# Retention and gated FFN on one core: attention steps joined to five groups in the 256-token blocks, weight sums moved to the first steps, the v casts of steps 3 to 8 from GpSimd to ScalarE

## The chip, the core and the metric

The kernel runs on one core of one Trainium2 chip. The core has TensorE (PE in the profile; PEld is its loading of weights), VectorE (DVE), ScalarE (ACT), GpSimd (POOL) and SyncE (SP), which only issues transfers. Each engine works through its own instructions in the order in which the program put them and waits at semaphores for the others. The metric is the time of one execution on the device in microseconds (us).

## The reference

```python
def _attn_ref(q, k, v):                      # q, k, v: 8 batches, 8 heads, 576 positions, 64
    scores = scale * np.matmul(q, k.transpose(0, 1, 3, 2))
    gamma = 1.0 - 2.0 ** (-5.0 - np.arange(H))
    Dmat = np.where(rel >= 0, gamma[:, None, None] ** rel[None, :, :], 0.0)
    return np.matmul(scores * Dmat[None, :, :, :], v)

def _moe_ref(x, w_gate, w_val, w_out):       # x: 4608 tokens x 512; d_ff 1536
    gate = 1.0 / (1.0 + np.exp(-(x @ w_gate)))
    return gate * (x @ w_val) @ w_out
```

Attention without softmax, with a decay that only depends on the distance, gives x; x goes through a gated feed-forward layer.

## The kernel before, in words

**Attention in steps.** The decay is put into tables that multiply q and k, so that within 128 positions the scores need only a triangular mask, and what lies further back is carried in a state. The first 768 token columns are made in pairs. The others are made in 30 *steps* `s` (`STEPS`), 128 columns each: step `s` makes columns 768+128s and on. For each step the loads of k, q and v go out on SP (`load_part`, L170, L173), k and q are multiplied with their tables (`cast_qk`, L425, POOL), v is cast to bf16 (`cast_v`, L430), and q and k together are transposed by a transfer (`cross`, L434, tile `T`; SP) or, for the steps in `TURNED` (0, 1, 7), by TensorE (`turn_step`, L616). On TensorE, `scores` (L654) and `products` (L662) of a step fill the tiles `row`; the DVE masks them (`mask`, L669, tile `pt`) and adds up the state (L784 to L790), which ACT casts (`sb`, L631). Later `intra` (L680) and `inter` (L695) of the same step fill the tiles `val`, and ACT copies these into `xT` (L756, L776). All of these are matmuls of 64x64. A `mark` (L703) is two tiny matmuls between those of one kind and the next.

**The feed-forward layer in blocks.** `BLOCKS` are two blocks of 256 token columns (from 512 and from 768), then blocks of 512. A 256 block has 18 units `i`: 12 of `h_units` (L896; `h_g_0`, `h_v_0`, `h_g_2` up to `h_v_10`), 8 matmuls of 128x256 each, then 6 of `op_units` (L1236; tiles `op_0` and `op_1`), 4 matmuls of 128x512 each. ACT takes the sigmoid of each `h_g` (L899), the DVE multiplies the `h_v` into it (L901), ACT copies each `op` out (L928). The `h` tiles go round three PSUM banks, so an `h` unit waits until ACT or the DVE has read the tile three before it. The block from 768 reads the x of steps 0 and 1; the first 512 block reads that of steps 2 to 5, and its sums (`x_sums`, L978) too.

**The order.** It is written out by hand. After each unit of a block the main loop puts down one thing: a piece of what is pending of an attention group, or the next group. Before, `next_slot(s)` put down single groups in the 256 blocks, with the values of step s-1 and the scores of step s (`slot`): steps 0 to 3 in the block from 512, 4 and 5 in that from 768, and then one joined group `slot_of_two` with the values of step 5 and the scores of steps 6 and 7. Each group was followed by its copies and state sums (`after`) as pending pieces and by the casts of a later step (`casts_to`), which also issue loads. `SUMS_AT` says after which units the DVE makes one of the sums of weights that the 512 blocks need.

Of the kernel before, what the change touches and what calls it, by code (L numbers as in the profile page):

```python
# [16 lines left out]
def kernel(  # L17
# [629 lines left out]
    def scores(s, banks=None):  # L647
        t = turned[s]
        row_ps[s] = [pool.tile([P, 2, M, 64], FP32, tag=tag, name=f"row_{s}_{i}")
                     for i, (pool, tag) in enumerate(banks or ROWS)]  # L650
        for m in range(M):
            for y in range(2):
                for j in range(NJ):
                    nc.tensor.matmul(row_ps[s][y][half(j), 0, m, :], lhsT=t[half(y), 1, m, half(j)],  # L654
                                     rhs=t[half(y), 0, m, half(j)], start=True, stop=True, skip_group_check=True)
# [16 lines left out]
    def values(n, name):  # L672
        return [pool.tile([P, n, 64], FP32, tag=tag, name=f"val_{name}_{i}") for i, (pool, tag) in enumerate(VALS)]

    def intra(s, begins=True):
        for kc in range(M):
            for j in range(NJ):
                for x in range(2):
                    h = 2 * kc + x
                    nc.tensor.matmul(val_ps[s][j][half(x), kc, :], lhsT=natural["v", s][half(j), h, :],  # L680
                                     rhs=probs[s][half(j), h // M, h % M, :], start=(begins and kc == 0),
                                     stop=(kc == M - 1),
                                     skip_group_check=True)

    def inter(s, js):


        for u in range(2):
            for y in range(2):
                for j in js[y]:  # L690
                    if before(s, j) is None:
                        continue
                    for x in range(2):
                        m = 2 * u + x
                        nc.tensor.matmul(val_ps[s][j][half(x), 2 * y + u, :], lhsT=before(s, j)[half(y), m, :],  # L695
                                         rhs=turned[s][half(y), 0, m, half(j)], start=False, stop=(u == 1),
                                         skip_group_check=True)

    def mark(pool, tag, **more):

        t = pool.tile([P, 64], FP32, tag=tag, name="mark", **more)
        for y in range(2):
            nc.tensor.matmul(t[half(y)], lhsT=blank[half(y), half(y)], rhs=blank[half(y), half(y)], start=True, stop=True)  # L703

    def slot(s):

        if s > 0:
            val_ps[s - 1] = values(M, s - 1)
            intra(s - 1)
            inter(s - 1, [(0,), (1,)])  # L710
            mark(st_psum, "st")
        scores(s)
        if STEPS[s][1] < LAST:
            products(s)
        if s > 0:
            mark(st_psum, "st")
            inter(s - 1, [(1,), (0,)])
        mask(s)

    ROWS_2 = [(st_psum, "st"), (ffn_psum, "ffn")]  # L720
    glance = consts.tile([P, NJ], FP32)

    def slot_of_two(vals, news):


        if vals:
            both = values(len(vals) * M, vals[0])
            for i, s in enumerate(vals):
                val_ps[s] = [t[:, i * M:(i + 1) * M] for t in both]
                intra(s, i == 0)  # L730
                inter(s, [(0,), (1,)])
            if len(news) == 2:
                mark(*ROWS_2[0])
            else:
                for j in range(NJ):
                    nc.scalar.copy(out=glance[:, j:j + 1], in_=both[j][:, 0, 0:1])
        for s, banks in zip(news, (ROWS, ROWS_2)):
            scores(s, banks)
            if STEPS[s][1] < LAST:
                products(s)  # L740

        def rest():
            for s in vals:
                inter(s, [(1,), (0,)])

        if not news:
            return rest
        rest()
        for s in news:
            mask(s)  # L750
# [19 lines left out]
                    if (s, j) in totals:  # L770
                        keep_state((b, c, j), totals.pop((s, j)), on_act)

    def leave_x(s, j):

        cols = cols_of(s, j)
        nc.scalar.copy(out=x_out(ALL, cols), in_=x_in(val_ps[s][j], cols))  # L776

    def add_state(s, j):

        b, c = STEPS[s]  # L780
# [8 lines left out]
        else:  # L789
            nc.vector.tensor_copy(out=new, in_=p)  # L790
        running[b] = totals[s, j] = new

    def after(s, i):

        makes = STEPS[s][1] < LAST
        to_bf16 = on_act if s < 6 else on_pool
        if i == 0:
            if makes:
                add_state(s, 0)
        else:  # L800
            if s > 0:
                leave_x(s - 1, i - 1)
                if i == 2 and dealt(cols_of(s - 1, 0)):
                    x_sums(at_col[s - 1], False)
            if i == 1 and makes:
                add_state(s, 1)
            if makes and (s, i - 1) in totals:
                b, c = STEPS[s]
                keep_state((b, c, i - 1), totals.pop((s, i - 1)), to_bf16)


    def first_batch_state():

# [17 lines left out]
    def casts_to(s):  # L831
        while done["cast"] <= min(NS - 1, s):
            x = done["cast"]
            loads_to(3 * (x + 1 + (AHEAD[x] if x < len(AHEAD) else 2)))
            cast_qk(x, 1, nc.gpsimd)
            cast_qk(x, 0, nc.vector if x < 2 else nc.gpsimd)
            if x not in TURNED:
                cross(x)
            cast_v(x, on_dve if x == 0 else on_pool)
            done["cast"] += 1  # L840

    cast_part = [0]
# [2 lines left out]
    def next_cast():  # L845
# [15 lines left out]
        n = 3 * x + i - LOADS["begin"] + 1  # L861
        loads_to(min(LOADS["begin"] + n + 12, LOADS["loaded"] + n + n // 3))
        cast_part[0] = (i + 1) % 3

    def next_slot(s):
        slot(s)
        casts_to(s + LEAD_CAST)
        for i in range(3):
            pending.append(lambda i=i: after(s, i))
        if s + 1 == 1:  # L870
            pending.insert(2, lambda: turn_step(s + 1))

    def next_two(vals, news, late):
        rest = slot_of_two(vals, news)
# [206 lines left out]
        return quarter  # L1081

    PLACES = (((1, 1), "g", 0), ((1, 2), "w", 0), ((2, 1), "w", 1), ((2, 2), "g", 1))
    TURN_AT = -1
    JOINED = "g0 w0 g1 w2".split()
    BY_DVE = "w01 w00".split()
    BY_DVE_LAST = "w00".split()
# [437 lines left out]
    weight_sums = [lambda kind=kind, u=u, i=i: w_sums(kind, i, u, nc.vector) for kind, u in (("g", 2), ("w", 2)) for i in (0, 1, 2, 3)]  # L1525
    weight_sums += [lambda u=u, i=i: wo_sums(i, u, 3) for u in range(3) for i in (0, 1, 2, 3)]

    SUMS_AT = {0: (1,3,5,7,8,9,11,12,13,14,15,16,17), 1: (1,3,4,5,7,9,11)}
    SPARE = {}
    for at, kind, u in PLACES:  # L1530
        SPARE.setdefault(at, []).append(lambda kind=kind, u=u: w_sums(kind, 2, u, nc.vector))
    SINGLE = [4, 2]
    pieces = 0
    slots = 0
    valued = -1
    for w, (t0, n) in enumerate(BLOCKS):
        nxt = BLOCKS[w + 1] if w + 1 < len(BLOCKS) else None
        last = last_step(nxt[0] + nxt[1]) if nxt else NS - 1
        end = slots + (SINGLE[w] if w < len(SINGLE) else 0)
        begin = slots  # L1540
        total = 2 * NFC * 4 * n + 12 * 512 * (n // P)
        n_h = NFC if n <= 256 else 2 * NFC
        if n == 512:
            n_h = 0
        gone = 0
        twos = []
        at = end
        while not twos and valued + (end - begin) < last or twos and twos[-1][0][-1] < last:
            vals = list(range((twos[-1][0][-1] if twos else valued + end - begin) + 1, at))
            twos.append((vals, list(range(at, min(at + 2, NS)))))  # L1550
            at = min(at + 2, NS)
        if w < 1:
            twos = []

        for i, cols in enumerate(ffn_units(t0, n, nxt)):
            if i in SUMS_AT.get(w, ()) and weight_sums:
                weight_sums.pop(0)()
            if w == 1 and i == n_h + TURN_AT:
                turn_step(7)
            for x in SPARE.get((w, i - n_h if w == 1 else i), ()):  # L1560
                x()
            gone += cols
            pieces += 1
            if w == 2 and i in (24, 32):
                keeps[0] -= 1
                leave()
            if stores and (nxt is None or w + 2 == len(BLOCKS) and pieces % 4 == 0):
                leave()
            if n > 256 and i % 2 and i < n_h:
                continue  # L1570
            if pending:
                pending.pop(0)()
            elif slots < end and gone * (end - begin) >= (slots - begin) * (total - 5 * 2048):
                next_slot(slots)
                valued = slots - 1
                slots += 1
            elif twos and (cue if n == 512 else i - n_h >= 1):
                cue.clear()
                next_two(*twos[0], n == 512)
                valued = twos[0][0][-1]  # L1580
                slots = max([slots] + [s + 1 for s in twos.pop(0)[1]])
        assert not twos and slots >= end
        while pending:
            pending.pop(0)()
    while stores:
# [30 lines left out]
```

## Time and profile before

| | us |
|---|---|
| runs | 305.58 median of 3 (304.92, 305.58, 307.17) |
| the profiled execution | 305.17 |
| its span, from the first to the last instruction of the program | 303.5 |
| start of the block from 512 in the chain of waits | 52.43 |
| start of the block from 768 | 71.54 |
| start of the first 512 block | 90.33 |

The span's clock starts with the first instruction; 1.67 us of the profiled execution lie around it. A row of the chain of waits counts a run of matmuls from the end of the one before it where they follow each other without a break, so that successive rows add up; a row of the timeline begins where the first of the matmuls began, up to 0.2 us earlier, since they overlap.

### The profile page before, as it was taken

How to read it: one execution, taken by the hardware profiler on the slowest of the kernel's cores; microseconds unless marked ns; L12 is line 12 of the kernel's file. 1: busy time of each engine (PE TensorE's matmuls, PEld its weight loads, DVE VectorE, ACT ScalarE, POOL GpSimd, SP SyncE). 2: the span in 40 equal slices, each digit the busy share in tenths (PEclk: the TensorE clock that was granted, in tenths of full speed). 3: DMA queues.
4: the chain of work that ended last, by engine and by line, in shares of the span. 5: the costliest groups of instructions: out<-in, count | busy, mean ns of one | idle time of the engine just before them, and what ended most of it. 6: DMA issues, size and time to landing. Idle time of an engine off the chain costs nothing.

```text
span 303.5 us, 10861 instructions
## 1 busy us (share of the span) xinstructions
PE 295.1 (97%) x4433; PEld 243.6 (80%) x4442; DVE 243.8 (80%) x476; ACT 197.1 (65%) x422; POOL 209.5 (69%) x255
## 2 busy tenths in 40 slices
PE   7899999999999999999999999999999999999994
PEld 6764455876858888888888888888888888888883
DVE  5956996787887899689978997898789968946793
ACT  6755463545548656965796579657965886648640
POOL 4776563655367899769976997699769916741670
PEclk9999999999999999999999999999999999999999
DMA  7999999999999995999589929994970390012004
GB/s 214 291 361 402 364 301 215 192 221 177 143 245 211 234 254 133 245 233 248 120 209 244 193 58 196 224 221 65 223 171 2 106 246 3 2 60 84 1 2 138
DMA packets 144994, 55.01 MB, mean 181 GB/s; under 512 B 124336, under 2 KB 136880, under 8 KB 144944
## 3 DMA queue, kind: packets, MB, share of 16 engines
q1 hardware_dynamic: 144144, 53.66, 74.3%
q8 instruction: 35, 0.57, 0.8%
q10 hardware_dynamic: 800, 0.66, 0.7%
q14 instruction: 15, 0.12, 0.1%
HBM read 37.75 MB, written 9.44 MB: 155 GB/s over the span
## 4 chain that ended last, share of the span: by engine, by line
PE 90%; SPq 4%; DMA 2%; DVE 1%; issue 1%; POOL 0%
PE gatea L1020 12%; PE wa L1020 12%; PE qa L1134 11%; PE qe L1134 9%; PE gatee L1020 6%; PE we L1020 6%; PE h_v L896 4%; PE h_g L896 4%; PE op L1476 3%; PE op L1236 3%; PE gateg L1020 3%; SPq L184 3%; PE wg L1020 3%; PE hv L1326 3%; PE hg L1326 3%; PE val L680 2%
## 5 line engine op out<-in xcount | busy, mean ns | idle before, releaser
L425 POOL TENSOR_TENSOR qk<-k,ktab 128x512 bf16<-128x512 f32 x30 | 32.2, 1072 | 17.0 <-DMA k<-in_k_dram 13.7
L1134 PEld LDWEIGHTS <-gsum 128*128 128x128 bf16 x336 | 31.9, 98 | 5.0 <-DVE gsum L957 0.8
L957 POOL TENSOR_TENSOR gsum<-gv 128x256 bf16<-128x256 bf16 (+1 forms) x35 | 26.5, 765 | 12.3 <-DVE gv L1045 11.1
L1020 PEld LDWEIGHTS <-wg_sb 128*128 128x128 bf16 x308 | 30.1, 98 | 3.7
L1020 PEld LDWEIGHTS <-wv_sb 128*128 128x128 bf16 x308 | 30.1, 98 | 3.5
L425 POOL TENSOR_TENSOR qk<-q,qtab 128x512 bf16<-128x512 f32 x28 | 30.7, 1095 | 2.2 <-DMA q<-in_q_dram 2.1
L1020 PEld LDWEIGHTS <-wvt 128*128 128x128 bf16 x280 | 27.4, 98 | 3.2
L1020 PEld LDWEIGHTS <-wgt_sb 128*128 128x128 bf16 x252 | 24.7, 98 | 2.9
L669 DVE TENSOR_TENSOR pt<-row,tri 128x256 bf16<-128x256 f32 x60 | 21.5, 414 | 6.8 <-PE row L662 3.2
L1134 PEld LDWEIGHTS <-gv 128*128 128x128 bf16 x240 | 23.0, 98 | 3.0
L957 POOL TENSOR_TENSOR gsum<-gv,gsum 128x256 bf16<-128x256 bf16 x37 | 25.4, 716 | 0.0
L1045 POOL TENSOR_TENSOR gv<-gv,wu 128x512 bf16<-128x512 bf16 x7 | 8.1, 1163 | 24.2 <-DVE wu L1071 24.2
L631 ACT CAST sb<-s 128x256 bf16<-128x256 f32 x46 | 18.3, 414 | 5.0 <-DVE s L788 3.9
L1020 PE MATMUL wa<-xsum,wv_sb 128*128 128x256 bf16 x140 | 21.0, 273 | 0.0
L1020 PE MATMUL gatea<-xsum,wg_sb 128*128 128x256 bf16 x140 | 19.9, 273 | 0.0
L1045 POOL TENSOR_TENSOR gv<-gv,ws 128x512 bf16<-128x512 bf16 x15 | 17.5, 1164 | 2.8 <-DVE ws L1074 2.8
L1074 DVE TENSOR_TENSOR gs<-gatea,gs 128x512 f32<-128x512 f32 x21 | 13.9, 688 | 6.1 <-PE gatea L1020 5.2
L756 ACT CAST xT<-val 128x256 bf16<-128x256 f32 x50 | 15.8, 390 | 4.6 <-PE val L695 4.6
L430 POOL CAST v<-v 128x512 bf16<-128x512 f32 x20 | 14.1, 704 | 6.3 <-DMA v<-in_v_dram 6.3
L1074 DVE TENSOR_TENSOR ws<-wa,ws 128x512 f32<-128x512 f32 x21 | 14.4, 686 | 4.1 <-PE wa L1020 4.1
L1043 ACT ACTIVATE gv<-gs 128x512 bf16<-128x512 f32 x21 | 13.0, 630 | 6.9 <-DVE gs L1074 6.8
L1066 DVE TENSOR_TENSOR gatee<-gatea,gs 128x512 f32<-128x512 f32 x14 | 9.8, 700 | 9.5 <-PE gatea L1020 6.6
(183 smaller groups left out, 861.8 us busy)
## 6 DMA issues: line engine op xcount, KB each, us to landing
k<-in_k_dram SPq DMA_DIRECT2D x26, 256.0 KB, 4.3
q<-in_q_dram SPq DMA_DIRECT2D x26, 256.0 KB, 4.0
v<-in_v_dram SPq DMA_DIRECT2D x26, 256.0 KB, 4.3
out_dram<-ob SPq DMA_DIRECT2D x25, 256.0 KB, 3.3
wg<-in_moe_w_gate_dram SPq DMA_DIRECT2D x12, 256.0 KB, 5.3
wv<-in_moe_w_val_dram SPq DMA_DIRECT2D x12, 256.0 KB, 5.2
wo<-in_moe_w_out_dram SPq DMA_DIRECT2D x12, 256.0 KB, 4.9
v32p<-in_v_dram SPq DMA_DIRECT2D x6, 256.0 KB, 4.6
```

Source lines behind the costliest of these rows:

```text
L425: eng.tensor_tensor(out=natural_qk[s][:, i].rearrange("p m (y d) -> p y m d", y=2), in0=by_halves(loaded[s][1 - i]), in1=tab, op=ALU.mult)
L430: eng(out=natural["v", s], in_=loaded[s][2])
L631: eng(out=state[key], in_=src)
L669: nc.vector.tensor_tensor(out=probs[s][:, y], in0=row_ps[s][y][:, 0], in1=tri.unsqueeze(1).to_broadcast([P, M, 64]), op=ALU.mult)
L756: nc.scalar.copy(out=x_out(ALL, cols_of(s, i)), in_=x_in(val_ps[s][i], cols_of(s, i)))
L896: nc.tensor.matmul(ps[:, i], lhsT=w_sb[:, kc, (fc + i) * P:(fc + i + 1) * P], rhs=xT(kc, slice(t0, t0 + n)), start=(kc == 0), stop=(kc == ...
L957: eng.tensor_tensor(out=to, in0=a, in1=b, op=op)
L1020: nc.tensor.matmul(ps[:, f], lhsT=w[:, kc, f * P:(f + 1) * P], rhs=x[:, kc], start=(first and f == 0 and kc == 0), stop=(f == 1 and kc == ...
L1045: eng.tensor_tensor(out=to, in0=to, in1=src, op=ALU.mult)
L1074: nc.vector.tensor_tensor(out=me["s5"], in0=a, in1=me["s5"], op=ALU.add)
L1134: nc.tensor.matmul(ps[:, b], lhsT=left(fp)[:, b * P:(b + 1) * P], rhs=right(fp), start=(first and fp == 0 and b == 0), stop=(fp == NFC // ...
L1326: nc.tensor.matmul(ps, lhsT=(wg_sb if what == "g" else wv_sb)[:, kc, fc * P:(fc + 1) * P], rhs=xT(kc, slice(0, 4 * P)), start=(kc == 0), s ...
```

## The change

The single groups are gone. `EARLY` lists, for each of the two blocks, after which unit which values (`vals`) and scores (`news`) are put down together: five groups with ([], [0, 1]) and ([0, 1], [2, 3]) in the block from 512, and ([2, 3], [4]), ([4], [5]) and ([5], [6, 7]) in that from 768. `slot_of_two` now serves one new step as well, and in the last group of the program, which has values only, a `mark` stands where ACT had copied one column of `val` into `glance`. The step that TensorE turns first (1) and step 7 are put at fixed units by `TURN_AT`. In the table `SUMS_AT` the first weight sums of the block from 512 stand after units 0 to 5. `casts_to` gives `cast_v` of steps 3 to 8 to ACT.

```diff
     def slot_of_two(vals, news):
...
-            if len(news) == 2:
-                mark(*ROWS_2[0])
-            else:
-                for j in range(NJ):
-                    nc.scalar.copy(out=glance[:, j:j + 1], in_=both[j][:, 0, 0:1])
-        for s, banks in zip(news, (ROWS, ROWS_2)):
+            mark(*ROWS_2[0])
+        for s, banks in zip(news, (ROWS, ROWS_2 if vals else VALS)):
             scores(s, banks)
             if STEPS[s][1] < LAST:
                 products(s)
+        if vals and len(news) == 1:
+            mark(*ROWS_2[0])
 
         def rest():
+            if not news:
+                mark(*ROWS_2[0])
             for s in vals:
                 inter(s, [(1,), (0,)])
...
-            cast_v(x, on_dve if x == 0 else on_pool)
+            cast_v(x, on_dve if x == 0 else on_act if 2 < x < 9 else on_pool)
...
-    TURN_AT = -1
+    TURN_AT = ((1, (0, 3)), (7, (1, 11)))
...
-    SUMS_AT = {0: (1,3,5,7,8,9,11,12,13,14,15,16,17), 1: (1,3,4,5,7,9,11)}
+    SUMS_AT = {0: (0, 1, 2, 3, 4, 5, 11, 12, 13, 15, 16, 17), 1: (0, 1, 3, 4, 5, 7, 9, 11)}
...
-    SINGLE = [4, 2]
+    EARLY = (((6, [], [0, 1]), (13, [0, 1], [2, 3])), ((2, [2, 3], [4]), (7, [4], [5]), (13, [5], [6, 7])))
...
-            elif slots < end and gone * (end - begin) >= (slots - begin) * (total - 5 * 2048):
-                next_slot(slots)
-                valued = slots - 1
-                slots += 1
-            elif twos and (cue if n == 512 else i - n_h >= 1):
+            elif early:
+                if i >= early[0][0]:
+                    _, vals, news = early.pop(0)
+                    next_two(vals, news, False)
+                    valued, slots = ([valued] + vals)[-1], news[-1] + 1
+            elif twos and cue:
                 cue.clear()
-                next_two(*twos[0], n == 512)
+                next_two(*twos[0], True)
```

What the change moves shows best on ACT. At the end of the block from 512 ACT's rows stood like this before; `op_0` is the first output tile of that block, `val_0` and `val_1` are the two value tiles of one step (first of step 1, then of step 2), `xT` is x.

```order
L899 ACTIVATE gv_2_1402<-h_g_10_1519 128x2x256
L776 CAST xT_1396<-val_0_1426 128x4x64
L631 CAST sb_0_0_1545<-s_2_0_0_1529 128x256
L776 CAST xT_1396<-val_1_1427 128x4x64
L631 CAST sb_0_1_1554<-s_2_0_1_1543 128x256
L928 COPY ob_1647<-op_0_1547 128x512
L776 CAST xT_1658<-val_0_1561 128x8x32
```

At the same place they now stand like this; the four copies of `val_0` and `val_1` are those of steps 0 and 1.

```order
L851 ACTIVATE gv_2_1338<-h_g_10_1369 128x2x256
L430 CAST v_1555<-v_4_1315 128x512
L430 CAST v_1571<-v_5_1548 128x512
L880 COPY ob_1577<-op_0_1390 128x512
L740 CAST xT_1579<-val_0_1401 128x4x64 x2
L740 CAST xT_1579<-val_1_1402 128x4x64 x2
L631 CAST sb_0_0_1594<-s_2_0_0_1582 128x256
```

The casts of the v of steps 4 and 5 have come to stand ahead of the copy of `op_0` and of all copies that make the x of the block from 768. In the middle of that block ACT's rows before were these, from the sigmoid of `h_g_6` on.

```order
L899 ACTIVATE gv_1_1820<-h_g_6_1843 128x2x256
L899 ACTIVATE gv_2_1956<-h_g_8_1957 128x2x256
L776 CAST xT_1658<-val_0_1853 128x8x32
L631 CAST sb_3_0_1970<-s_2_3_0_1954 128x256
L776 CAST xT_1658<-val_1_1854 128x8x32
L899 ACTIVATE gv_2_1956<-h_g_10_1984 128x2x256
```

Now they are these.

```order
L851 ACTIVATE gv_1_1783<-h_g_6_1812 128x2x256
L430 CAST v_1919<-v_7_1756 128x512
L851 ACTIVATE gv_2_1921<-h_g_8_1922 128x2x256
L740 CAST xT_1776<-val_0_1833 128x8x32
L740 CAST xT_1776<-val_1_1834 128x8x32
L631 CAST sb_3_0_1949<-s_2_3_0_1933 128x256
```

The cast of the v of step 7 stands between the sigmoids of `h_g_6` and `h_g_8`. On POOL the six casts are gone and nothing else has moved; on SP the order of the transfers is as it was.

More of the change, by code (lines that the diff above doesn't have):

```diff
@@ L703, in mark @@
             nc.tensor.matmul(t[half(y)], lhsT=blank[half(y), half(y)], rhs=blank[half(y), half(y)], start=True, stop=True)
[L705 to L718, printed above, removed]
     ROWS_2 = [(st_psum, "st"), (ffn_psum, "ffn")]
-    glance = consts.tile([P, NJ], FP32)
     def slot_of_two(vals, news):
@@ L771, in after_two @@
                         keep_state((b, c, j), totals.pop((s, j)), on_act)
-    def leave_x(s, j):
-        cols = cols_of(s, j)
-        nc.scalar.copy(out=x_out(ALL, cols), in_=x_in(val_ps[s][j], cols))
     def add_state(s, j):
@@ L791, in add_state @@
         running[b] = totals[s, j] = new
[L793 to L809, printed above, removed]
     def first_batch_state():
@@ L863, in next_cast @@
         cast_part[0] = (i + 1) % 3
[L865 to L871, printed above, removed]
     def next_two(vals, news, late):
@@ L1538 @@
         last = last_step(nxt[0] + nxt[1]) if nxt else NS - 1
-        end = slots + (SINGLE[w] if w < len(SINGLE) else 0)
-        begin = slots
-        total = 2 * NFC * 4 * n + 12 * 512 * (n // P)
+        early = list(EARLY[w]) if w < len(EARLY) else []
         n_h = NFC if n <= 256 else 2 * NFC
@@ L1544 @@
             n_h = 0
-        gone = 0
         twos = []
-        at = end
-        while not twos and valued + (end - begin) < last or twos and twos[-1][0][-1] < last:
-            vals = list(range((twos[-1][0][-1] if twos else valued + end - begin) + 1, at))
+        at = slots
+        while not early and (not twos and valued < last or twos and twos[-1][0][-1] < last):
+            vals = list(range((twos[-1][0][-1] if twos else valued) + 1, at))
             twos.append((vals, list(range(at, min(at + 2, NS)))))
             at = min(at + 2, NS)
-        if w < 1:
-            twos = []
         for i, cols in enumerate(ffn_units(t0, n, nxt)):
@@ L1557 @@
                 weight_sums.pop(0)()
-            if w == 1 and i == n_h + TURN_AT:
-                turn_step(7)
+            for step, turn_at in TURN_AT:
+                if turn_at == (w, i):
+                    turn_step(step)
             for x in SPARE.get((w, i - n_h if w == 1 else i), ()):
                 x()
-            gone += cols
             pieces += 1
@@ L1572 @@
                 pending.pop(0)()
-            elif slots < end and gone * (end - begin) >= (slots - begin) * (total - 5 * 2048):
-                next_slot(slots)
-                valued = slots - 1
-                slots += 1
-            elif twos and (cue if n == 512 else i - n_h >= 1):
+            elif early:
[4 more added lines that the diff above has]
+            elif twos and cue:
                 cue.clear()
-                next_two(*twos[0], n == 512)
+                next_two(*twos[0], True)
                 valued = twos[0][0][-1]
                 slots = max([slots] + [s + 1 for s in twos.pop(0)[1]])
-        assert not twos and slots >= end
+        assert not twos and not early
         while pending:
```

## The prediction

> **What bounds the kernel now.** I read the page first, for the shares of the engines, with the rows of its first part:
>
> ```profile
> span 303.5 us, 10861 instructions
> ...
> PE 295.1 (97%) x4433; PEld 243.6 (80%) x4442; DVE 243.8 (80%) x476; ACT 197.1 (65%) x422; POOL 209.5 (69%) x255
> ```
>
> PE is nearly always at work, so a change gains only what it takes off PE, and loses whatever makes PE stand still. Next I read the busy times by stage: the block from 512, that from 768, and two blocks of 512 (columns: the stretch, its length, busy us and instructions of PE, PEld, DVE, ACT, POOL, the granted clock, DMA share, GB/s).
>
> ```profile
> 52.30:71.40 19.10, 18.89 (x356) 14.22 (x357) 15.92 (x37) 9.95 (x24) 11.96 (x13) 1.00 1.05 197
> 71.40:90.20 18.80, 18.59 (x346) 14.16 (x347) 14.52 (x32) 8.48 (x20) 9.57 (x11) 1.00 1.15 199
> 90.20:120.40 30.20, 30.20 (x490) 26.75 (x489) 26.46 (x50) 21.41 (x46) 26.06 (x32) 1.00 0.96 209
> 120.40:150.70 30.30, 30.30 (x507) 26.97 (x505) 25.39 (x49) 22.64 (x50) 25.39 (x30) 1.00 0.94 210
> ```
>
> In the two blocks that are rewritten, 52 to 90 us, PE is full, ACT and POOL are half empty, and the DMA engines are full (a share above 1, as transfers overlap). The first 512 block takes as long as the second (30.2 and 30.3), so there is nothing after 90 us in which a delay could be made good. Third, the chain of waits in order of time (start, length, what):
>
> ```profile
> 52.43 0.87 PE h_g L896 x8
> 53.68 0.98 PE h_v L896 x8
> ...
> 62.02 0.87 PE h_v L896 x8
> 63.73 0.98 PE h_g L896 x8
> ...
> 71.54 0.87 PE h_g L896 x8
> 73.11 0.98 PE h_v L896 x8
> 74.09 0.87 PE h_g L896 x8
> ...
> 77.59 0.87 PE h_g L896 x8
> ...
> 82.78 0.87 PE h_v L896 x8
> 83.66 0.45 PE turn L616 x8
> ...
> 90.33 0.87 PE gatea L1020 x8
> ```
>
> From 52.43 to 90.33, 37.90 us, PE alone sets the pace. Four units from 74.09 to 77.59 give 0.875 us each; 36 units are 31.5, the two turns 0.9, and 5.5 us are left for the seven attention groups.
>
> **The change part by part: the joined groups.** A group is priced from these rows. Step 0's single group lies between the end of `h_g_0` (53.30) and the start that a unit of 0.87 ending at 53.68+0.98=54.66 would have (53.79): 0.49 us for 32 small matmuls. Step 4's lies between 72.41 and 73.22: 0.81 for 68. The joined one lies after the turn (84.11) and two `op` units (85.86) and ahead of four more, which end at 90.33: 0.97 for 98. The line through the first and the last is 0.26 us a group and 7.3 ns a matmul. Counted from the code, the seven groups have 32, 68, 68, 60, 68, 68 and 98 matmuls, 462; by the line 5.2 us, against 5.5 found (step 2's took 62.89 to 63.84, 0.95, so a wait is in it). The five new ones have 64, 130, 92, 68 and 98, 452: 5*0.26+452*0.0073=4.6 us. Taken alone, that is a gain of 0.6 to 0.9; I take 0.8. About 1.0 of it falls in the block from 512 (0.73 and 1.21 instead of 0.49, 0.81, 0.95 and 0.73), and 0.1 is given back in that from 768 (0.93 instead of 0.81).
>
> **The casts of v.** These are POOL's rows for steps 3 to 8, in order, with the idle time before each and what ended it:
>
> ```profile
> 60.58 0.60 POOL L430 CAST v<-v 128x512 bf16<-128x512 f32 x1
> ...
> 65.55 0.60 POOL L430 CAST v<-v 128x512 bf16<-128x512 f32 x1
> ...
> 71.12 0.69 POOL L430 CAST v<-v 128x512 bf16<-128x512 f32 x1 [1.06 <-DMA v<-in_v_dram]
> ...
> 77.36 0.61 POOL L430 CAST v<-v 128x512 bf16<-128x512 f32 x1 [1.22 <-DMA v<-in_v_dram]
> ...
> 83.90 0.61 POOL L430 CAST v<-v 128x512 bf16<-128x512 f32 x1 [2.12 <-DMA v<-in_v_dram]
> ...
> 88.13 0.61 POOL L430 CAST v<-v 128x512 bf16<-128x512 f32 x1 [0.33 <-DMA v<-in_v_dram]
> ```
>
> From step 5 on POOL waited for the load itself. The wait moves with the cast to ACT, and there it has work behind it that PE needs. Do the loads come sooner now? These are SP's rows for the v of steps 5 and 7:
>
> ```profile
> 65.48 1.12 SPq L170 DMA_DIRECT2D v<-in_v_dram  x1
> ...
> 77.34 1.07 SPq L170 DMA_DIRECT2D v<-in_v_dram  x1
> ```
>
> The share of the DMA engines that SP's queue took from 56 to 90 us:
>
> ```profile
> q1 hardware_dynamic: 26610, 6.68, 111.1%
> ```
>
> And POOL's group of k multiplies from 52 to 91 us, with its idle time and what ended it:
>
> ```profile
> L425 POOL TENSOR_TENSOR qk<-k,ktab 128x512 bf16<-128x512 f32 x8 | 8.5, 1068 | 10.0 <-DMA k<-in_k_dram 6.6 <-PE val L695 1.8 <-PE mark L703 1.6
> ```
>
> SP's order is unchanged and its engines are full. POOL sat idle 10.0 us ahead of its k multiplies, so the 3.7 us of six casts taken off it make no q, and no transpose that SP waits to send, any sooner. I take the landings as they were: 71.1 for step 5, 83.9 for step 7. What a cast and what follows it take on ACT is in its timeline:
>
> ```profile
> 68.99 0.58 ACT L928 COPY ob<-op 128x512 f32<-128x512 f32 x1 [1.51 <-PE op L1236]
> 69.47 0.38 ACT L776 CAST xT<-val 128x256 bf16<-128x256 f32 x1
> ...
> 81.07 0.60 ACT L899 ACTIVATE gv<-h_g 128x512 bf16<-128x512 f32 x1 [1.98 <-PE h_g L896]
> ...
> 116.73 1.20 ACT L756 CAST xT<-val 128x256 bf16<-128x256 f32 x4
> ...
> 123.75 0.61 ACT L430 CAST v<-v 128x512 bf16<-128x512 f32 x1
> 124.25 0.59 ACT L1002 COPY gs<-gatee 128x512 f32<-128x512 f32 x1
> ```
>
> The next instruction begins 0.50 us after a cast of v, 0.48 after a copy of an `op`; four copies to `xT` take 1.20.
>
> *At the block from 768:* v of step 5 begins at 71.12, the copy of `op_0` at 71.62, the `xT` copies at 72.10, and they end at 73.30. Only then can `h_g_0` begin; after a break the first unit takes 0.98, so it ends at 73.35+0.98=74.33, where it ended at 71.54+0.87=72.41: 1.9 us later. PE, 1.0 us ahead by the joined groups, would have been ready at 70.5 and stands still for 2.8.
>
> *At step 6* nothing binds: PE ends `h_g_4` at 74.33+1.75+0.93+1.75=78.76, and ACT, after the cast at 77.36 and two copies, is free at 78.4.
>
> *At step 7:* the cast begins at 83.90, the sigmoid of `h_g_8` behind it at 84.40, and ends at 85.00. `h_v_10` needs the bank of `h_g_8`, so it ends at 85.05+0.98=86.03, where it ended at 82.78+0.87=83.65: 2.4 us later. PE would come there 1.9+0.1=2.0 late anyway, so this wait adds 0.4. Each of the two waits alone thus gives about 2.
>
> *At step 8:* the cast at 88.13 is over before `op_0` of that block ends (87.7 before, now 90.1), and costs nothing. Steps 3 and 4 had landed by 60.6 and 65.5, when ACT has nothing else ready.
>
> From `h_v_10` on to 90.33 PE has the same units, turn and group as before, so the first 512 block begins 2.4 late, and by the stages above the end does too.
>
> That ACT doesn't pass over a waiting instruction is to be seen in the first two of ACT's rows, with this one of PE:
>
> ```profile
> 67.76 0.23 PE L695 MATMUL val<-T,sb 64*64 64x64 bf16 x3
> ```
>
> The values of step 2 were complete at 68.0, but ACT, standing before `op_0` until 68.99, copied the first of them at 69.47. The sum with such waits is +2.4; if ACT could pass the cast over, it would be -0.8. The Trainium skill, PSUM — Partial Sum Buffer, "Engine vs sequencer instructions", calls the queues of ScalarE, VectorE and GpSimd strict first-in first-out. By that rule the sum is +2.4 as well, and the trace agrees, with 1.5 us of waiting for a copy whose input was there.
>
> **The rest** I cost at nothing. The weight sums moved forward are on the DVE, which has 3 us free in the block from 512 and is ahead of ACT's wait there. The last group's four tiny matmuls are 0.03 us of PE, for two copies off ACT; either could turn out 0.1 the other way.
>
> The sum: 305.17 + 2.4 = 307.6. The profiled execution lies 0.4 under the median of the runs; from the median it is 308.0. I say 307.8. For the unknowns, the landings may differ by half a microsecond from execution to execution: +1.9 to +2.9.
>
> **The rivals.** *No wait, so faster.* If v of step 5 were there by 68.3 (70.5 less 2.2 of ACT's work) and that of step 7 by 80.8, only the joined groups would count: -0.8, 304.8 from the median. Speaking for it: nothing after 52 us lets PE depend on those loads now, so their time is known from one execution alone. Against: both would have to land 2.8 and 3.1 us sooner, from full DMA engines and an unchanged order. Chance 0.10.
>
> *Loads sooner by 1 to 1.5 us*, because SP or the engines run more freely without some delay that I can't see: both waits shrink alike, +0.9 to +1.4, 306.7. Chance 0.18.
>
> *Loads later by about 1 us.* Nothing here takes it up, unlike before: +3.4, 309.0. Chance 0.12.
>
> *The clock falls while PE stands still.* The granted clock was 1.00 in all stretches above, and in this one at the start, in which PE was idle for 1.4 of 5 us:
>
> ```profile
> 5.00:10.00 5.00, 3.62 (x64) 3.14 (x65) 2.78 (x5) 3.03 (x6) 2.08 (x2) 1.00 1.03 307
> ```
>
> A pause of 2.8 in one piece is not in this trace. If the clock were halved after it, two to four units of 0.875 would take twice as long, of which the wait of step 7 (0.4) would hide a part: +1.4 to +3.1 on top, 309.4 at the least. Chance 0.10. The Trainium skill, TensorE: Matmul & The Clock Gate, "What's actually happening", states half rate after an idle window of about 3.4 us. By that rule a pause of 2.8 keeps the clock, and the sum stays +2.4; a load of step 5 that came 0.6 later would lose it. No run here shows which.
>
> **How the numbers follow.** The forecast, both waits as worked out, has 0.50; it is the likeliest, so the time is 307.8. The forecast, the sooner and the later loads hold 0.80 together, and the range is theirs: from 306.0, the sooner loads' +0.9 on the profiled 305.17, to 309.3, the later ones' 309.0 and a little for the spread of a median of three, short of the fallen clock's 309.4. One per cent, 3.06 us, is about what a measurement of this kernel can tell from no change. Faster by more than that: no case reaches it, 0.02. Slower by more, above 308.6: the clock, most of the later loads and the tail of the forecast, 0.22. Within it: 0.76.
>
> **What would show it.** ACT's row of the v cast of step 5 with some 5 us of idle time ended by its load, ahead of the copy of `op_0`; PE idle for 2.8 us before the first `h_g` of the block from 768, released by ACT's `xT`; ACT idle for 2 to 3 us before the v cast of step 7, and a short stop of PE at `h_v_10`; the first `gatea` at 92.7; POOL's waits for k unchanged. I am wrong if v of steps 5 and 7 lands well before 71 and 83.9, if PE's pause lies elsewhere, if the clock is below 1.00 after it, or if the 512 blocks take other than 30.3.

## The result, and the profile after

Over 19 runs of each, the changed kernel takes 307.75 us in the median (305.29 to 310.78) and the kernel before 305.47 (304.22 to 307.59). The ratio is 1.0069, with a 95% interval of 1.0047 to 1.0091: slower by 2.3 us. The ratio leaves out one run of the changed kernel, 310.78 us, which lies over 1.5% above its fastest one. The forecast was 307.8, within 306.0 to 309.3.

The profiled execution is one of the longer ones, 309.81 us with a span of 308.1. First its page, the answer to the two rows of before: PE has 2.2 us more of busy time and works a smaller share of a longer span, and POOL has six instructions less.

```profile
span 308.1 us, 10850 instructions
...
PE 297.3 (96%) x4427; PEld 245.3 (80%) x4436; DVE 245.0 (80%) x476; ACT 199.9 (65%) x426; POOL 204.6 (66%) x249
```

Its busy time by stage, with the same columns as before (stretch, length, busy us and instructions of PE, PEld, DVE, ACT and POOL, granted clock, DMA share, GB/s):

```profile
52.30:71.40 19.10, 17.95 (x320) 13.68 (x321) 17.21 (x36) 7.59 (x16) 10.30 (x10) 1.00 1.09 199
71.40:92.70 21.30, 18.94 (x361) 14.46 (x362) 14.09 (x32) 12.71 (x32) 9.09 (x9) 0.92 1.00 201
92.70:122.90 30.20, 30.20 (x483) 26.01 (x481) 26.30 (x49) 22.60 (x51) 22.69 (x27) 1.00 0.85 186
```

The first 512 block takes 30.2 us, full of PE, as before. The loss is in the two 256 blocks, and in the second row the granted clock is 0.92. The chain of waits says what they wait for:

```profile
60.81 10.67 DMA v<-in_v_dram x2
...
71.55 0.47 issue
72.03 0.58 ACT ob L880
72.61 1.11 ACT xT L740 x4
...
73.76 1.29 PE h_g L848 x8
75.05 1.71 PE h_v L848 x8
76.75 1.45 PE h_g L848 x8
...
94.69 0.87 PE gatea L972 x8
```

Where PE alone had set the pace, there is now a load of v, the cast, the copy of `op_0` and the four `xT` copies, and then three units that take 1.29, 1.71 and 1.45 instead of 0.98, 0.87 and 0.87: 1.73 us lost to the clock. The casts of v in ACT's timeline, steps 4 to 7 (start, length, what, idle time before and what ended it), with what follows step 5's:

```profile
66.45 0.62 ACT L430 CAST v<-v 128x512 bf16<-128x512 f32 x1 [2.72 <-DMA v<-in_v_dram]
71.50 0.62 ACT L430 CAST v<-v 128x512 bf16<-128x512 f32 x1 [4.44 <-DMA v<-in_v_dram]
72.03 0.58 ACT L880 COPY ob<-op 128x512 f32<-128x512 f32 x1
72.51 1.20 ACT L740 CAST xT<-val 128x256 bf16<-128x256 f32 x4
...
78.73 0.61 ACT L430 CAST v<-v 128x512 bf16<-128x512 f32 x1
...
83.35 0.61 ACT L430 CAST v<-v 128x512 bf16<-128x512 f32 x1
```

And the two stops in PE's timeline:

```profile
67.47 0.32 PE L654 MATMUL row<-T 64*64 64x64 bf16 x16 [0.94 <-DMA T<-qk]
...
73.76 0.49 PE L848 MATMUL h_g<-xT,wg_sb 128*128 128x256 bf16 x3 [2.15 <-ACT xT L740]
```

The wait of step 5's cast is there as forecast, at 71.50 for 71.12. That of step 7 is not: its cast starts without idle time. And there is a stop that the prediction didn't have: the second joined group (called group B below) waits 0.94 us for the transposed q and k of step 3.

In what follows, the three stages are compared by the first rows of their units in PE's timeline: the first `h_g` of the block from 512, the first `h_g` of that from 768, the first `gatea`. In the first profile of before these lie at 52.27, 71.38 and 90.17, so the blocks take 19.11 and 18.79 us, 37.90 together.

### The profile page after: what moved, and what is told of

Read it like the earlier page. It is cut to its first block, busy times and chain, and to the rows that moved or that the text cites. A ratio compares the mean times of both kernels' runs of the same rounds, so it can differ in the third digit from the quotient of the medians.

```text
span 308.1 us, 10850 instructions
## 1 busy us (share of the span) xinstructions
PE 297.3 (96%) x4427; PEld 245.3 (80%) x4436; DVE 245.0 (80%) x476; ACT 199.9 (65%) x426; POOL 204.6 (66%) x249
## 3 DMA queue, kind: packets, MB, share of 16 engines
HBM read 37.75 MB, written 9.44 MB: 153 GB/s over the span
## 4 chain that ended last, share of the span: by engine, by line
PE 73%; DMA 15%; SPq 3%; DVE 3%; POOL 2%; issue 1%; ACT 1%; POOLq 0%; DVEq 0%
PE gatea L972 12%; PE wa L972 11%; PE qa L1086 11%; PE qe L1086 9%; PE gatee L972 6%; PE we L972 6%; DMA v<-in_v_dram 5%; DMA wg<-in_moe_w_gate_dram 4%; DMA v32p<-in_v_dram 3%; PE gateg L972 3%; PE wg L972 3%; PE h_g L848 2%; PE h_v L848 2%; SPq L184 2%; DMA k32p<-in_k_dram 2%; PE val L680 2%
## 5 line engine op out<-in xcount | busy, mean ns | idle before, releaser
L669 DVE TENSOR_TENSOR pt<-row,tri 128x256 bf16<-128x256 f32 x60 | 21.3, 412 | 4.9 <-PE row L662 2.9
L740 ACT CAST xT<-val 128x256 bf16<-128x256 f32 x60 | 18.9, 389 | 5.7 <-PE val L695 5.7
L767 DVE TENSOR_TENSOR s<-s,row 128x256 f32<-128x256 f32 x39 | 16.2, 416 | 0.9
```

The costliest lines, as they stand in the source:

```text
L669: nc.vector.tensor_tensor(out=probs[s][:, y], in0=row_ps[s][y][:, 0], in1=tri.unsqueeze(1).to_broadcast([P, M, 64]), op=ALU.mult)
L740: nc.scalar.copy(out=x_out(ALL, cols_of(s, i)), in_=x_in(val_ps[s][i], cols_of(s, i)))
L767: nc.vector.tensor_tensor(out=new, in0=running[b], in1=p, op=ALU.add)
```

## The experiments

**A second and third profile of the changed kernel, and a second of before.** First: is the pause a property of the kernel or of that one execution, and does the clock belong to it?

> The changed kernel, unchanged, for a second profile; the first was of a run at granted clock 0.992. If the loss is the wait for v_5's load (theory), the pause before the first h_g of block 768 is there again, 1.5 to 2.5 us and released by ACT's xT, and block 2 begins 39.5 to 40.5 us after the first unit of block 512 where the clock stays at 1.00 (38.1 in the kernel before), 41 to 42.5 where it falls; the run then takes about 307.5 or about 309. If the pause belonged to the one profiled run (rival), it is under 0.5 us here and the run takes 305.5 or less.

> The changed kernel once more, for a third profile. The theory expects the same as of the second: a pause of 1.5 to 2.5 us before the first h_g of block 768, and the first three units after it at 0.9 to 1.0 us each with the clock at 1.00, or 1.3 to 1.7 us each where it has fallen. The rival that the fall of the clock is no consequence of the pause expects units that are slow also without the pause, or none slow in either profile.

> The kernel before once more, for a second trace. The prediction took the landings of v from one execution: 71.1 for step 5, 83.9 for step 7. If 83.9 belonged to that execution, step 7 lands near 81 here, as in the five kernels run since (80.0 to 81.2), and step 5 within 0.5 of 71. If it belongs to the order of before, it lands near 84 again.

The two executions of the changed kernel took 307.87 and 307.78, at clocks of 0.998 and 1.000; that of before 305.76, at 1.000. PE's timeline of the first:

```profile
52.33 1.04 PE L848 MATMUL h_g<-xT,wg_sb 128*128 128x256 bf16 x8
...
67.41 0.32 PE L654 MATMUL row<-T 64*64 64x64 bf16 x16 [0.70 <-DMA T<-qk]
...
73.67 1.03 PE L848 MATMUL h_g<-xT,wg_sb 128*128 128x256 bf16 x8 [2.12 <-ACT xT L740]
74.53 1.04 PE L848 MATMUL h_v<-xT,wv_sb 128*128 128x256 bf16 x8
...
92.69 1.04 PE L972 MATMUL gatea<-xT,wg_sb 128*128 128x256 bf16 x8
```

And of the second:

```profile
52.54 1.04 PE L848 MATMUL h_g<-xT,wg_sb 128*128 128x256 bf16 x8
...
65.11 1.89 PE L1188 MATMUL op<-wo_sb,gv 128*128 128x512 bf16 x8 [0.39 <-DVE gv L853]
...
73.75 1.03 PE L848 MATMUL h_g<-xT,wg_sb 128*128 128x256 bf16 x8 [1.84 <-ACT xT L740]
...
92.77 1.04 PE L972 MATMUL gatea<-xT,wg_sb 128*128 128x256 bf16 x8
```

The pause is there each time. The load of step 5's v lands at 71.4 to 71.5, and `h_g_0` starts at 73.7 to 73.8, whatever PE lost or saved before it: 0.94 and 0.70 us of waiting for T in two executions, 0.39 for the DVE in the third. That block is set by the load. At full clock the two blocks take 21.34+19.02 = 40.36 and 21.21+19.02 = 40.23; in before's second profile 19.29+18.79 = 38.08. Against the two profiles of before that is 2.2 to 2.5 us, the whole of the loss. Five of the 19 runs of the changed kernel took only 305.3 to 306.5 us; no such run was profiled, so how long the pause was in them is open.

Before's second profile also tells whose landing the 83.9 of step 7's load was: it came at 83.3 there, so the late landing belongs to the kernel before and not to one execution of it.

Only the first profile shows slow units after the pause.

**The casts back on POOL, the five groups kept.**

```diff
-            cast_v(x, on_dve if x == 0 else on_act if 2 < x < 9 else on_pool)
+            cast_v(x, on_dve if x == 0 else on_pool)
```

> The five joined groups and the moved weight sums, with the v casts of steps 3 to 8 left on POOL. If the waits of ACT for the v loads carry the loss, they are gone here: the gain of the joined groups (0.6 to 0.9) remains, less a wait of up to 0.9 for the transpose of step 3, which the changed kernel's trace shows at the second group: -0.9 to +0.1 against before, and the granted clock 1.00 throughout. If the joined groups themselves cost the time, it stays at +2.

305.21 us (12 runs) against 305.24, ratio 0.9994, interval 0.9971 to 1.0017. The loss is gone, and no gain takes its place. PE's timeline:

```profile
51.96 1.04 PE L848 MATMUL h_g<-xT,wg_sb 128*128 128x256 bf16 x8
...
67.06 0.32 PE L654 MATMUL row<-T 64*64 64x64 bf16 x16 [0.69 <-DMA T<-qk]
...
71.03 1.04 PE L848 MATMUL h_g<-xT,wg_sb 128*128 128x256 bf16 x8
...
90.07 1.04 PE L972 MATMUL gatea<-xT,wg_sb 128*128 128x256 bf16 x8
```

The blocks take 19.07 and 19.04, together 38.11, against 37.90 and 38.08 of before. What the joined groups save in the first block, group B gives back for the most part by waiting 0.69 us for T of step 3, and the second block is 0.25 longer than before.

**The casts alone, in the kernel before.**

```diff
-            cast_v(x, on_dve if x == 0 else on_pool)
+            cast_v(x, on_dve if x == 0 else on_act if 2 < x < 9 else on_pool)
```

> The kernel before, with only the v casts of steps 3 to 8 put on ACT, at the places where POOL had them in the program. If a cast holds up everything behind it on ACT until its load has landed, this is worse than the change: the cast of step 5 (71) stands ahead of the sigmoid of h_g_10 of the block from 512, and that of step 7 (80.7 to 83.9) ahead of the sigmoid of h_g_2 of the block from 768, which began at 75.0 before: +6 to +9. If what costs is ACT's own work for the casts (6 of 0.6) or the places in the joined groups, +2 or less.

311.89 us (4 runs), ratio 1.0202, interval 1.0166 to 1.0237: 6.6 us slower. The chain of waits has two loads of v with ACT's cast behind them:

```profile
56.19 4.71 DMA v<-in_v_dram
60.92 0.62 ACT v L430
...
72.88 4.04 DMA v<-in_v_dram
77.00 0.62 ACT v L430
```

These are the loads of steps 3 and 6. ACT stood 4.55 us before step 3's cast, with the sigmoid of an `h_g` behind it, and a stop of 2.23 us in PE follows, with a fallen clock (below). In this profile (312.45 us) the two blocks take 42.66 us, 4.6 to 4.8 more than before, of which the clock has 1.7; another 2.1 to 2.6 were lost ahead of them, where the clock fell in the first 20 us as well. All four runs have a clock of 0.994 or less. So the forecast of +6 to +9, made from the waits alone, was met with the clock's help. That ACT's casts cost time without the joined groups too is shown; that these take the worst of it away, since in the changed kernel the casts stand between other work, is a likely reading that no run tests by itself.

**The cast of step 5 alone moved.** The changed kernel, with this one cast put down together with that of step 6; the engine is still ACT.

```diff
-            cast_v(x, on_dve if x == 0 else on_act if 2 < x < 9 else on_pool)
+            if x == 5:
+                put_off.append(x)
+            else:
+                while x == 6 and put_off:
+                    cast_v(put_off.pop(), on_act)
+                cast_v(x, on_dve if x == 0 else on_act if 2 < x < 9 else on_pool)
```

> The changed kernel with the ACT cast of the v of step 5 put further back, ahead of that of step 6, so that the copies that make the x of the block from 768 stand ahead of it. The same engines do the same work. If the place of that one cast makes the pause, the pause of about 2.2 and the fall of the clock go, and the wait for step 7 decides what is left: with its v at 80.7, as in the changed kernel's trace, -0.5 to 0 against before; at 83.9, as in the trace of before, +1.5 to +2. If ACT's load of work or the groups make it, +2.3 stays.

305.54 us (12 runs), ratio 0.9998, interval 0.9971 to 1.0025. ACT's timeline:

```profile
67.74 0.59 ACT L887 COPY ob<-op 128x512 f32<-128x512 f32 x1 [2.03 <-PE op L1195]
68.23 1.21 ACT L740 CAST xT<-val 128x256 bf16<-128x256 f32 x4
...
80.03 0.62 ACT L430 CAST v<-v 128x512 bf16<-128x512 f32 x1 [1.50 <-DMA v<-in_v_dram]
```

And PE's first row of the block from 768:

```profile
70.13 1.04 PE L855 MATMUL h_g<-xT,wg_sb 128*128 128x256 bf16 x8
```

The copy of `op_0` now waits for PE, and the `xT` copies follow at 68.23 instead of 72.51. PE doesn't stop before `h_g_0`. Step 7's cast does wait 1.50 us for its load here, and PE doesn't stop for that either. The two blocks take 38.12 us together, as before. Six casts on ACT therefore cost nothing that is measured; the place of one of them costs 2 us. The clock is another matter: three of the twelve runs have one of 0.994 without this pause.

**The second group one unit later** (casts on POOL): does the wait for T hide the gain of the joined groups?

```diff
-    EARLY = (((6, [], [0, 1]), (13, [0, 1], [2, 3])), ((2, [2, 3], [4]), (7, [4], [5]), (13, [5], [6, 7])))
+    EARLY = (((6, [], [0, 1]), (14, [0, 1], [2, 3])), ((2, [2, 3], [4]), (7, [4], [5]), (13, [5], [6, 7])))
```

> Casts on POOL and the five groups, with the second group one unit later (after unit 14 of the block from 512), when the transpose of step 3 has landed. If the wait of 0.5 to 0.9 for that transpose is what takes the gain of the joined groups, it goes and the time is 0.5 to 0.8 below before. If the groups gain nothing, the time stays that of before, -0.2 to +0.2.

305.32 us (12 runs) against 305.35, ratio 0.9989, interval 0.9966 to 1.0013. In the trace the wait is gone:

```profile
52.13 1.04 PE L848 MATMUL h_g<-xT,wg_sb 128*128 128x256 bf16 x8
...
70.49 1.04 PE L848 MATMUL h_g<-xT,wg_sb 128*128 128x256 bf16 x8
...
89.71 1.04 PE L972 MATMUL gatea<-xT,wg_sb 128*128 128x256 bf16 x8
```

The block from 512 takes 18.36 us, 0.75 to 0.93 less than in the two profiles of before, so the gain of the joined groups is real. The block from 768 takes 19.22, 0.4 more. Both together are 37.58, 0.3 to 0.5 less than before, which the times of these runs can't tell from nothing.

**Both edits together** (casts on ACT with step 5's later, and the later group), a version that might beat both kernels.

> Five groups, the second of them one unit later, and ACT's cast of v_5 put down with that of v_6. The wait for T of step 3 took 0.5 to 0.9 in the runs that had the second group at unit 13, and none with it at 14; the place of v_5's cast took the pause away. Theory: both are gone, block 2 begins 37.4 to 37.8 us after the first unit of block 512 against 38.1 before, so the time is 0.3 to 0.7 us under the kernel before, ratio 0.9975 to 0.9990, too little to be told from no change. Rival: with ACT's casts the later group finds v or T late and the stop comes back there, ratio 1.000 or above.

> The kernel with both edits once more, for a second profile: in the first, blocks 512 and 768 took 37.75 us together as expected, but the twelve times had a median of 306.58. If the time over the kernel before comes from a clock that fell in the first 20 us (as in the first profile, where the first unit of block 512 began 2.2 to 2.4 us late), blocks 512 and 768 take 37.4 to 38.0 us again, and the first unit of block 512 begins at 51.8 to 52.4 with the clock at 1.00 in the first 20 us and the run under 305, or at 54 and the run at 306 or more. If it comes from ACT's casts (rival), the two blocks take over 38.5 us here, with a stop released by ACT or by a load of v.

306.58 us (12 runs), ratio 1.0037, interval 1.0005 to 1.0069: not faster, but a little slower. The two blocks took 37.75 in the first profile, as worked out, and 38.32 in the second, where PE waited 0.54 us for the DVE. The first profile lost its time far ahead of them, in the first 20 us, where PE waited for POOL's `vp` (PE's timeline, then the stretch):

```profile
14.30 0.38 PE L508 MATMUL st<-vp,kp 64*128 64x128 bf16 x4 [1.77 <-POOL vp L409]
```

```profile
10.00:20.00 10.00, 7.97 (x164) 6.23 (x162) 6.63 (x12) 5.43 (x11) 6.35 (x10) 0.83 0.96 277
```

The clock was 0.83 there, and the block from 512 began at 54.24 instead of 52. That part of the program is the same in all kernels here, so it gives no reason why this one should be slower on the whole; in the second profile, 306.05 us at clock 0.997, the same stop is 0.63 us and the clock stays. Four of the twelve runs have a clock of 0.994, but the eight others have a median of 306.46, so the clock doesn't explain it either. Why the median is 1 us above before stays open.

**The weight sums alone, in the kernel before.**

```diff
-    SUMS_AT = {0: (1,3,5,7,8,9,11,12,13,14,15,16,17), 1: (1,3,4,5,7,9,11)}
+    SUMS_AT = {0: (0, 1, 2, 3, 4, 5, 11, 12, 13, 15, 16, 17), 1: (0, 1, 3, 4, 5, 7, 9, 11)}
```

> The kernel before with only the weight sums moved to the changed kernel's units. The prediction cost this at nothing, since the DVE has 3 us free in the block from 512: -0.2 to +0.2. If the sums hold up the masks or the h_v products, +0.5 or more, with PE waiting for the DVE in the first units.

306.03 us (10 runs), ratio 1.0022, interval 0.9997 to 1.0048. One stop of PE is new in the trace:

```profile
59.26 0.31 PE L680 MATMUL val<-pt,v 64*64 64x64 bf16 x14 [0.57 <-DVE T L618]
```

DVE's sums ran ahead of its copy of T, which came at 58.79 instead of 57.16 in before's second profile. The two blocks took 38.68, 0.6 to 0.8 more than before. The times alone don't settle it, since the interval still holds 1. With the five groups (casts on POOL) that stop isn't there.

**The pause filled with matmuls**, to separate the clock from the wait: 18, then 44 matmuls of 128x128 on a constant tile at the end of the block from 512 of the changed kernel; they add work that no output uses.

```diff
+    def busy(n):
+        t = st_psum.tile([P, 4, P], FP32, tag="st", name="busy")
+        for _ in range(n):
+            nc.tensor.matmul(t[:, 0], lhsT=blank, rhs=blank, start=True, stop=True)
...
+            if w == 0 and i == 17:
+                busy(18)
```

> The changed kernel with 18 tiny matmuls of 128x128, which nobody reads, put on PE at the end of the block from 512, so that PE is at work for most of its pause (about 1.8 of 2.2). If the fall of the clock after the pause is a part of the loss, it goes: clock 1.00 in the units of the block from 768, 0.87 to 0.98 each, and a time 0.8 to 1.7 less than that of the change. If the fall belongs to the one profiled execution and the median does not have it, the time stays at +2.3 against before.

> As with 18 matmuls, but 44, about 2.9 us of them, so that PE has no pause of more than half a microsecond. If the low clock of 8 of the changed kernel's 19 runs (0.992 to 0.994) comes from the pause, no run is below 0.996 here and the runs above 308.5 go; the time is then the wait alone, +1.9 to +2.3, 307.2 to 307.6. If the clock falls for another reason, some four of ten runs stay below 0.995 and the spread is as before.

With 18: 307.89 us (12 runs), ratio 1.0060, interval 1.0028 to 1.0093, and four of the twelve at a clock of 0.992 to 0.994. With 44: 310.04 us (6 runs), ratio 1.0149, interval 1.0109 to 1.0190, none below 0.997. PE's timeline of the second:

```profile
69.68 2.62 PE L710 MATMUL busy<-blank 128*128 128x128 bf16 x44
72.95 1.03 PE L853 MATMUL h_g<-xT,wg_sb 128*128 128x256 bf16 x8 [0.65 <-ACT xT L745]
```

With 44 the pause shrank to 0.65 us, and `h_g_0` started no later than without them. That agrees with a wait that is set by the load, and with a clock that falls from the pause; but six runs without a low clock prove little where eight of nineteen had one, and where kernels without this pause had some too. The 18 took only 1.17 us and left a pause of 1.58, which is inconclusive. The kernel with 44 loses another 2 to 3 us after these blocks, in stops for which the trace has no cause, such as this one, so its time says nothing about the clock:

```profile
116.42 0.28 PE L1091 MATMUL qa<-wt_sb,gsum 128*128 128x256 bf16 x1 [0.57 <-issue]
```

## Why the prediction held, and which of its steps did not

| step of the prediction | forecast, us | found, us |
|---|---|---|
| step 5's cast holds `op_0` and `xT` up: block from 512 | +1.9 | +1.9 to +2.2 at full clock |
| wait of step 7's cast, in the block from 768 | +0.4 | none |
| joined groups, in the block from 768 | +0.1 | +0.2 |
| sum | +2.4 | +2.2 to +2.5 at full clock |
| clock after the pause | a rival | fell in the profiled run: 1.73 |

That the median came within 0.1 us of the forecast is partly luck: the +0.4 of step 7 is missing, and the runs with a low clock lift the median from 307.49 to 307.75.

**The cast of step 5.** The mechanism and its size were right. It was shown from both sides: with the cast elsewhere on the same engine the time is that of before, and with all six on POOL too. The prediction put PE's readiness at 70.5, and so the pause at 2.8; it came to 1.84 to 2.15, because PE had lost time to other waits in that block and was ready later. For the sum that made no difference, since the load sets the end of the block.

ACT worked in order, as the prediction took it: in the profiled run it stood 4.44 us before a cast, until 71.50, though the values for `xT` had been complete from 68.05 on. The Trainium skill, PSUM — Partial Sum Buffer, "Engine vs sequencer instructions", calls its queue strict first-in first-out, and these rows agree.

**Step 7: wrong.** "I take the landings as they were: ... 83.9 for step 7" failed. SP issued that load 1.0 us sooner (76.37 for 77.34), and it landed at 80.73. In the other profiles it landed at 80.0 to 82.8, later only in before's second profile (83.3) and with the weight sums alone (83.8). These are SP's rows in the two kernels, before first; the transpose ahead takes 2.47 and 1.29 to issue, and then what follows moves up:

```profile
73.58 2.47 SPq L434 DMA_TRANSPOSE T<-qk  x1
...
77.34 1.07 SPq L170 DMA_DIRECT2D v<-in_v_dram  x1
```

```profile
73.79 1.29 SPq L434 DMA_TRANSPOSE T<-qk  x1
...
76.37 1.01 SPq L170 DMA_DIRECT2D v<-in_v_dram  x1
```

Why the transpose is issued faster wasn't tried. So the step that failed is that an unchanged order on SP means unchanged landings: the kernel before has 83.9 and 83.3, the changed one 80.7, 81.3 and 81.9, and either the groups (80.4, casts on POOL) or the casts (81.2, seven groups) gave an earlier landing by themselves. The sentence that each of the two waits alone gives about 2 us isn't borne out: the one of step 5 gave it all, and with that one gone waits of 1.50 and 1.94 at step 7 cost PE nothing. What a landing at 83.9 would have cost no run shows.

**The joined groups: mis-sized where they matter.** Forecast were 1.0 us less in the block from 512 and 0.1 more in that from 768. The three profiles with the second group one unit later show 0.6 to 0.9 less, and those of the five groups 0.2 to 0.4 more in the block from 768 (0.6 and 1.1 with both edits, where PE also waits for the DVE); there the group of 92 matmuls took 1.03 to 1.15 us instead of the 0.93 of the line. With the casts on POOL 0.69 of the gain is lost again in the wait for T of step 3, which the prediction didn't look for: the group at unit 13 came to that T at 66.37 and it landed at 67.02; in before the single group came at 67.39 and it had landed at 66.16. Hence about 0 where the casts are on POOL. In the changed kernel none of this shows, since the load sets the end of that block; the forecast's +1.9 had already taken that in.

**The weight sums at nothing:** as far as seen right for the changed kernel, where the casts on POOL alone bring back the time of before; the waits of 0.17 and 0.39 for the DVE in its third profile are hidden by the load. In the kernel of seven groups they cost a stop of 0.57 us.

**The clock: an outcome beside the forecast, not instead of it.** It was a rival with a chance of 0.10. Of the 19 runs, 8 had a clock of 0.992 to 0.994 and a median of 308.8 us; the 11 others 307.49, which is 2.0 over before. Of the 70 runs of before next to the experiments, 7 had a clock of 0.994 or less, with a median of 307.27 against 305.26 for the others. The whole run's clock doesn't tell where it fell, and the first 20 us can lower it too, so not all eight need be due to the pause. Two counts speak for caution: the two kernels with step 5's cast later have no such pause and yet 7 of 24 runs with a clock of 0.994, and the three with the casts on POOL (the five groups at both places, and the weight sums alone) have 2 of 34. What makes the difference isn't shown.

## What to carry to other kernels

An operation that waits for a load belongs on an engine that has nothing urgent behind it, or behind that urgent work on its engine: look at what stands behind the waiting instruction, not at how busy the engine is. Joining work saves little where it makes a consumer earlier than its operand; look for the transfer that the joined group needs first. A landing time read from the kernel before needn't hold after the change, even where the order of the transfers stays: step 5's load landed at 70.2 to 72.2 us in all profiles, but step 7's at 83.3 to 83.9 before and at 80.7 to 81.9 in the changed kernel.

## What the runs showed of the hardware

The granted clock fell after some pauses of PE of 1.3 to 2.2 us, and not after all of them. The casts-only kernel had a stop of 2.23 us ahead of 62.09 (PE's timeline) and then this stretch, with a unit of 1.89 us:

```profile
62.09 1.03 PE L896 MATMUL h_v<-xT,wv_sb 128*128 128x256 bf16 x8 [2.23 <-ACT gv L899]
...
64.59 1.89 PE L896 MATMUL h_g<-xT,wg_sb 128*128 128x256 bf16 x8
```

```profile
60.00:70.00 10.00, 7.70 (x177) 6.15 (x177) 6.28 (x12) 5.33 (x12) 4.51 (x5) 0.83 1.10 216
```

A clock of 0.83 over 10 us is 1.7 us lost, and so are 0.83 in the stretch with the pause of 1.77 above, and 0.92 over 21.3 us after the pause of 2.15. A narrower stretch of the changed kernel's first profile shows the fall itself:

```profile
74.40:77.80 3.40, 3.40 (x18) 2.35 (x16) 0.94 (x2) 1.51 (x4) 1.53 (x2) 0.50 0.94 208
```

In the 3.4 us on either side the clock is 1.00. The other falls look the same: 0.50 from 63.15 to 66.56 and, after a pause of 1.27, from 15.36 to 18.78 in the casts-only kernel, and from 15.86 to 19.27 in the one with both edits. So each fall on record lasts 3.4 us at half the clock and costs 1.7 us, and it begins 0.6 to 1.6 us after its pause has ended. After the changed kernel's pauses of 2.12 and 1.84 the clock stayed at 1.00, so the length of the pause alone doesn't decide. Nor does PE's busy time over 3.4 us: it was 1.64 ahead of the fall at 15.86, and 1.56 from 71.61 to 75.02 in the changed kernel's third profile, where no fall followed.

The Trainium skill, TensorE: Matmul & The Clock Gate, "What's actually happening", tells of half rate after an idle window of about 3.4 us, with a window that runs freely of the program. The falls of 3.4 us at 0.50 agree with one such window at half rate, and falls in some executions of one kernel and not in others agree with a free-running window; that a pause must fill it doesn't agree, since the clock fell after 1.27 to 2.23 us here.
